# One layer's kernel on one core: shift constants turned on PE, the last table's index made first, half of the h norms turned by DMA, one chain of roots for q, one PSUM ring of four

## The chip, the cores and the metric

The kernel runs on one core of a Trainium2 chip. A core has TensorE (PE, matrix products into PSUM), VectorE (DVE), ScalarE (ACT), GpSimd (POOL) and the queues that issue DMA transfers (SP's above all). Each engine works through its own instructions in order and waits on semaphores for the others. The metric is the device time of one execution in microseconds, smaller is better. Three runs of the kernel before gave 247.6 to 248.36 us, median 248.21 us.

## The reference

There are 2048 positions of 512 values. Stage A is a gated long convolution, stage B a mixer with an MLP. Everything is bf16 with sums in fp32.

```python
def _A_ref(q, k, v, shift_k, ssm_k, ssm_D):        # q comes in layer-normed
    for t in range(4):                              # four taps along the positions
        k_shift += k_pad[:, t:t + S, :] * shift_k[:, 3 - t]
    kv = k_shift * v
    y = irfft(rfft(kv, 2S) * rfft(ssm_k, 2S))[:S]   # a convolution of length 2048 for each channel
    return q * (y + kv * ssm_D)

h = x + _A_ref(_layernorm(x), k, v, ...)            # x is A_q

def _B_ref(x, w1, w2, w3, w4):                      # x is _layernorm(h)
    g = _gelu(_layernorm(x) @ w1)                   # 512 -> 512
    hs = shifted_by(-1, +1, -2, +2)(g quarters) @ w2
    x1 = x + hs
    return x1 + _gelu(_layernorm(x1) @ w3) @ w4     # 512 -> 1792 -> 512
out = h + _B_ref(_layernorm(h), ...)
```

## The kernel before, in words

The convolution is done as a Fourier transform written as matrix products. The channels come in two halves, cc = 0 and 1. The steps, with the names that the profile uses:

- **Front.** k, v and the long kernel (h, `hraw`) are loaded (`load_k`, `load_v`, `load_h`; 512 KB each, four of each) on SP's queue. PE first runs products of zeros (`pz`, `warm_up`) until k is there. `k_transposed` turns k on PE (`pk`) and an evacuation copies it to `kT`. `k_taps` applies the four taps on PE (`psh`) against diagonal matrices `dg`, and DVE multiplies by v on the way out (`kvq`, line 457). `k_rows` moves `kvq` by DMA into rows (`Rk`, line 464). `h_layout` turns the long kernel (`pt`, line 478), evacuated into `s` (`Rh`). `stage_a` is the first transform (`pah` of the kernel, `pak` of kv, line 494), evacuated into `T` (tile `ab`).
- **Tables.** POOL writes index grids (iota), POOL or DVE turn them into phases (`phase`), ACT takes sines. `WA` and `CSG` are small tables; `Wc` is a block-diagonal table, zeroed by 12 POOL memsets (line 385) and filled by 4 DMAs (line 388); `Wf` is the last table, made from an index `uf` (lines 394 to 398), which lies in the memory of `q_sb`, so q is loaded after the sines of `Wf` have read it (`qfree`, line 402; q loads at line 406). `Wf2` is `Wf` with its halves exchanged (`turned`, line 556).
- **Middle.** `stage_c` (`pc`, lines 518 to 520, three matmuls for each of 128 columns) needs all of `T` of its half and `Wc`. Its 32 PSUM tiles are evacuated into `s` (`xt`), DVE multiplies the transforms (`product`, line 641, and the sums at 655 and 657 into `Yr`, `Yi`). Then 16 groups of `pg` (line 721) go back, evacuated into `ab` (`Gs`). An evacuation can run on ACT or DVE (`evac`, lines 172 and 174). In between DVE takes the statistics of q (line 601, 16 instructions) and their inverse roots in two chains of eight columns each (`rsqrt_q`, `newton`).
- **Swap.** When all `Gs` are out, the PSUM pools of the front (rings `psa` and `psb`, two buffers each, taken in turn) close, and `psY` (2 buffers), `psT` (1) and `psW` (3) open. This is `mid`.
- **Tail.** `last_level` (`py`, line 774, eight) is evacuated by ACT, multiplied by the normed q and added to q by DVE (`gate`, lines 783 and 785), then statistics, roots (`rsqrt_h`) and norms (`norm_h`, line 812 on ACT, 815 on DVE) for blocks b = 0 to 3 of four position tiles. `on_pe` turns the normed tiles on PE (`pt2`, line 828, eight transposes for each pair) and an evacuation writes `xT`. Then w1 with GELU (`pw`, lines 840 and 844), w2 (`p2`, line 912), x1, statistics, roots, norms, again turned (`on_pe` for b = 0, `dma_start_transpose` at line 945 on SP's queue for the others), w3 with GELU, and w4 (`p4`, line 979) with the final sum (line 984) and the stores (line 989). Products of zeros (`pv`, `keep`) stand between the `py`.

The order is written out by hand: every step is added to a plan with a number, and `ISSUE` is the list of the numbers in the order in which they are issued, with a letter (A, V, G) where a step may run on more than one engine. Each engine keeps its part of this order. The plan's costs are not used when the kernel is built. Every DMA takes one of eight completion semaphores in turn and waits, at its place in its queue, until the last DMA of the same semaphore has landed.

Of the kernel before, what the change touches and what calls it, by code (L numbers as in the profile page):

```python
# [16 lines left out]
P = 128  # L17
S = 2048
# [5 lines left out]
DC = D // P  # L24
# [18 lines left out]
19 21 2 26 0 1 28 84 23 20 27 85 9 6 3 7 86 11 88 5 29 14 15 24 36 12 8 10 38 83 37 44 39 40 45 41 42 30G 31 17  # L43
22 25 81 87 46 43 32 18 95 34 16 47 92 96A 97V 94A 51 98 93V 89 105 91V 35 100A 54 49 133 99V 13 52 55 50 67 90A
101 33 134 48 63 136 106 102 138 103 104 4 56 64G 53 135V 137A 113 108 114 109 110 107 146 147A 58 116 57 141
156 142V 148 150 151V 157A 152 149A 153A 158 160 139 68G 161A 65 159V 143 261 154 69 112 140A 117 70 155V 115
111 118 166 145 167V 263 59 66 162 125 176 61 163A 62 174 366 177A 178 126 179A 164 172 175V 173V 182 165A 170
168 121 169V 122 183A 260 188 171A 189A 72 60 264 265A 76 75 73 221 220 74 215 218 219 216 214 217 230 231 232
233 80 79 190 228 192 191A 78 271 193A 272A 269 124 270A 186 127 266 184 267A 119 273 128 276 268 77 129 187A
185A 120 234 130 71 278 277A 281 279A 283 235 293 275 180 274 282A 284A 222 229 288 236 290 280 237 285 181A 295  # L50
289A 291A 123 238 287 239 294A 286 302 144 240 292 305 241 296A 210V 312 297 306V 242 262 303A 131 243 225 132
196 197A 202 200 208 201A 198 203A 199V 224 227 194 209A 204 195A 244 307 206 300 205A 207A 301A 223 226 318
308A 299 320 319A 298 313 315 245 304 309 310 321A 330 246 314A 332 311 316A 211A 247 325 327 322 331A 385 333A
317 248 328A 326A 367 324 323 373V 334 344 345A 342 337 343A 339 375V 329 338A 249 354 340A 336 356 351 335 250
349 346 371V 355A 341 374V 357A 352A 399 348 420 361 82 363 347 350A 395 369V 400A 251 396A 397 386 391 398A 358
393 353 360 359 212V 394V 387 392A 417 418V 388A 403 213V 252 404A 376V 405 406A 407 389 390V 409 408A 415 411
401 410A 416V 412A 402V 413 414A 419 446 253 254 440 255 368 256 257 258 259 454 441 370V 372A 379V 447A 377A
378A 448 449 450 452 455A 456 453 457 451 458 460 384A 459 461 499 500A 462 463 424 428 491 464 381A 492A 427
493 465 501 466 494 365 467 380A 438 495 468 496 469 470 502 471 472 503 505 477V 433 506 497 544 504 545A 498
507 508 430 473 383A 581 435 436 536 509 510 511 512 513 514 515 516 517 582A 425 434 537A 538 423 445 589 421  # L60
444 546 522V 439 478A 547 539 548 542 540 550 549 541 431 543 551 481 552 518 476A 475A 482A 362 426 553 554 442
432 382A 474 422 443 479 555 583 437 556 480A 429 489 520A 521A 524 487 485 523A 490 525A 364 519 488 486 557
558 559 770 560 526 527A 561 562 590A 584 483 568V 591 585 587 566V 586 592 588 593 484 595 594 532 596 597 598
599 528 533 600 629 529 530 601 567A 563 531 534 535 602 603 564 571 604 635 630 605 631 606 637 572A 565A 569
607 636 610V 570A 644 642 613V 632 633 634 638 640 639 645 643 641 646 647 648 649 650 651 573 579 574 577 575
652 653 580 611A 614 578 608 576 654 667 668 612A 655 669 615A 616 656V 617A 659V 664 666 657V 618 665 672 624
622 619 676 674 670 625 620 673 671 677 675 658A 662 623 678 679 626 680 621 609 699 681 663A 682 660 628 683
627 684 696 697 685 702 686 687 701 700 703 698 708 706 704 709 707 705 710 661A 781 782 779 773 780 774 688A
791 711 712 713 714 715 792 716 689 690A 717 785 787 731 691 718 719 732 733 771 738 739 786 740 789 741 752
692A 753 788 728 730 693 694A 695 790 772 754 724A 722A 797 798 726A 736 737 775 776 720A 755 729 734 817 818  # L70
756 757 825 826 758 759 827 828 725 829 735 833 830 834 760 742 823 824 723 761 743 777 778 793 794 766V 727 821
822 795 831 796 744 832 815 813 816 745 814 811 746 768V 812 783 784 721 747 819 835 836 820 805 800 853 847 748
859 749 854 848 809 860 810 871 750 851 751 762V 872 764V 852 769 861 804 799 867 763 873 862 868 869 767 874
# [59 lines left out]
def kernel(  # L133
# [23 lines left out]
    psa = front.enter_context(tc.tile_pool(name="psa", bufs=2, space=bass.MemoryType.PSUM))  # L157
    psb = front.enter_context(tc.tile_pool(name="psb", bufs=2, space=bass.MemoryType.PSUM))
    X = {"psa": psa, "psb": psb}
    plan = Plan({"psa": 2, "psb": 2, "psY": 2, "psT": 1, "psW": 3})  # L160
# [63 lines left out]
    def uf(hf):  # L224
        return X["q_sb"][:, 4 * hf:4 * hf + 4, :].rearrange("p a b -> p (a b)").bitcast(I32)
# [3 lines left out]
    ssk_bf = cst.tile([P, DC, 4], BF16)  # L229
# [20 lines left out]
    add({"A": 0.6}, lambda: nc.scalar.dma_start(ssk_bf[:], A_shift_k.rearrange("(c p) j -> p c j", p=P)), w=["sskb"], x=(0.6, 3.4))  # L250
# [5 lines left out]
    dma(0.6, lambda: nc.sync.dma_start(dcol[:], A_ssm_D.rearrange("(c p) -> p c", p=P)), w=["dcol"], x=(0.8, 2.5))  # L256
# [34 lines left out]
    add({"V": 0.5}, small, w=["warm", "mpi", "zero"])  # L291
    add({"V": 0.1}, lambda: V.memset(kT()[:, :, 26:32, 0:2], 0.0), r=("AB",), w=["kz"])
    add({"A": 0.3}, lambda: A.activation(warm[:], warm[:], ACT.Sin), r=["warm"], w=["sin"])
# [8 lines left out]
    def numbers():  # L302
# [10 lines left out]
    add({"V": 1.5}, numbers, r=["pidx"], w=["pf"], lock=True)  # L313
    v(2.2, lambda: V.tensor_tensor(
        out=dg().rearrange("p c j s -> p (c j) s"), in0=ident[:].unsqueeze(1).to_broadcast([P, 4 * DC, P]),
        in1=ssk_bf[:].rearrange("p c j -> p (c j)").unsqueeze(2).to_broadcast([P, 4 * DC, P]), op=MUL),
      ["id", "sskb", "AB"], ["dg"], lock=True)
# [33 lines left out]
    def hold():  # L351
        add({"G": 0.2}, lambda: G.tensor_tensor(out=gt[:], in0=CSG[:, 0:4], in1=dg()[:, 0, 0, 0:4], op=ADD),
            ["dg", "CSG"], ["gate"])
# [8 lines left out]
    sine(0.5, lambda: trc()[:, 1], uw, "uW", ("t", 1), False, ["AB"])  # L362
    add({"V": 0.2}, lambda: V.tensor_scalar(trc()[:, 2], trc()[:, 1], -1.0, None, op0=MUL),
        ["AB", ("t", 1)], [("t", 2)], lock=True)
    cosine(0.5, lambda: trc()[:, 0], uw, "uW", ("t", 0), ["AB"])
    for lo, hi, mult, off, key in ((0, 64, p64, 0.0, "uA"), (64, 81, k2X, 2048.0, "uG"), (81, 96, k2X, 0.0, "uH")):
        v(0.08, lambda lo=lo, hi=hi, mult=mult, off=off: V.tensor_scalar(
            um()[:, lo:hi], um()[:, lo:hi], mult, off, op0=MUL, op1=ADD), ["AB", "pf"], [key], lock=True)
    v(0.1, lambda: V.tensor_scalar(um()[:, 0:96], um()[:, 0:96], ANG - 1, None, op0=OP.bitwise_and),
# [5 lines left out]
    v(0.08, lambda: V.tensor_scalar(mk[:], i4[:], d4X, 1.0 / S, op0=OP.is_equal, op1=MUL), ["pf", "pidx"], ["mk"], lock=True)  # L375
    v(0.2, lambda: V.tensor_tensor(out=CSG[:].rearrange("p (n d) -> p n d", d=4),
# [3 lines left out]


    hold()
    for q in range(4):
        for a in range(3):
            add({"G": 0.95}, lambda q=q, a=a: G.memset(
                X["Wc"][:, q, a].rearrange("p d n k -> p (d n k)").bitcast(U32), 0), ["W", "gate"], [("wz", q, a)])
# [6 lines left out]
    for hf in range(2):  # L393
        iota(1.05, lambda hf=hf: uf(hf), [[1, 16], [32, 64]], 16 * hf, ("uf", hf), ["S1", "gate"])
        phase(0.75, lambda hf=hf: uf(hf), k1F, offF, ("uf", hf), ["S1"],
              after=[("wz", q, j) for q in range(4) for j in range(3)])
        sine(1.15, lambda hf=hf: Wf[:, 0, 16 * hf:16 * hf + 16, :].rearrange("p a b -> p (a b)"),
             lambda hf=hf: uf(hf), ("uf", hf), ("Wf", 0, hf), True, ["S1"])
# [3 lines left out]
    freed("qfree", [("uf", 0), ("uf", 1)])  # L402
    qd = A_q[0].rearrange("(n h t) d -> h n t d", h=2, t=NT)
    for tq in range(4):
        for h in range(2):
            dma(0.43, lambda h=h, tq=tq: nc.sync.dma_start(
                X["q_sb"][h * N1:(h + 1) * N1, 4 * tq:4 * tq + 4, :], qd[h][:, 4 * tq:4 * tq + 4, :]),
                r=["qfree"], w=[("q", h, tq)], x=(1.12, 2.5))

    def warm_up(n, x):  # L410
        key = ("pz", x)

        def pe():
            pz = psum("psb", key)
# [3 lines left out]
        add(mm(n), pe, ["zero"], [key, ("pzd", x)], opens=("psb", key))  # L418

    def k_transposed(qr):  # L420
# [10 lines left out]
        for cc in range(2):  # L431
            add({"A": 1.0, "V": 0.61},
# [593 lines left out]
```

## Time and profile before

| | us |
|---|---|
| median of three runs | 248.21 |
| the profiled execution, its own time | 247.9 |
| its span in the profile | 246.1 |
| PE, DVE, ACT, POOL busy | 229.4, 164.0, 155.5, 18.2 |
| first `pc` matmul | 41.20 |
| first `py` matmul | 95.43 |
| first `pw` matmul after which PE no longer waits | 118.02 |
| last `ob` sum on DVE (start) | 242.58 |

The span is 1.8 us shorter than the profiled execution's own time. A row of the profile gives start, duration, engine, source line, operation, output from input, and in brackets the idle time before it and who ended it. Instructions of ACT and DVE in a row overlap by about a tenth of a microsecond at their ends, so a row of seven that takes 6.61 us is a pitch of 0.94 us.

### The profile page before, as it was taken

The numbers are of one execution on the slowest core, as the hardware profiler recorded it, in microseconds if no ns is written. First come the engines' busy times: TensorE is split into PE (matmuls) and PEld (weight loads), VectorE is DVE, ScalarE is ACT, GpSimd is POOL, SyncE is SP. The second block draws the span as 40 slices with busy tenths as digits, with TensorE's granted clock in tenths as the row PEclk, the third lists the DMA queues.
The fourth block names the chain that finished last, engine by engine and source line by source line (L and its number), as shares of the span: only waits on it lengthen the run. The fifth ranks groups of instructions, "written<-read, shape, count | busy, mean of one in ns | idle before, by whom it ended". The sixth has DMA issues, their size and how long they took to land.

```text
span 246.1 us, 5097 instructions
## 1 busy us (share of the span) xinstructions
PE 229.4 (93%) x2108; PEld 151.0 (61%) x2108; DVE 164.0 (67%) x391; ACT 155.5 (63%) x203; POOL 18.2 (7%) x32
## 2 busy tenths in 40 slices
PE   8899899998798888988999999999999999999994
PEld 8899788997798875565445544444444444444542
DVE  6736878999999999999999999950150033003411
ACT  6704878999999999999956767863026402730000
POOL 4679100000000000000000000000000000000000
PEclk9999899999999999999999999999999999999999
DMA  6996868710000299000000004440120001101103
GB/s 196 376 407 163 239 198 184 166 50 4 0 3 0 65 355 348 8 0 0 3 0 0 4 1 86 85 87 3 27 48 10 3 15 28 43 3 43 32 21 75
DMA packets 18870, 20.77 MB, mean 84 GB/s; under 512 B 8608, under 2 KB 15392, under 8 KB 18848
## 3 DMA queue, kind: packets, MB, share of 16 engines
q1 hardware_dynamic: 18080, 20.32, 28.2%
q8 instruction: 16, 0.26, 0.5%
q10 hardware_dynamic: 768, 0.14, 0.3%
q14 instruction: 6, 0.05, 0.1%
HBM read 13.11 MB, written 2.10 MB: 62 GB/s over the span
## 4 chain that ended last, share of the span: by engine, by line
PE 63%; ACT 19%; DVE 12%; issue 2%; DMA 2%; SPq 0%; ACTq 0%
PE pw L840 23%; PE p L979 20%; ACT s L172 8%; ACT ab L172 5%; PE p L912 5%; PE psh L453 5%; PE pt L478 3%; DVE ab L174 3%; DVE kin L641 2%; PE pz L416 2%; ACT act L172 2%; DVE bst L597 2%; ACT ab L812 2%; DMA q_sb<-in_A_q_dram 2%; ACT act L844 1%
## 5 line engine op out<-in xcount | busy, mean ns | idle before, releaser
L840 PE MATMUL pw<-act,wts 128*128 128x512 bf16 x288 | 64.3, 379 | 1.1 <-ACT act L172 1.1
L844 ACT ACTIVATE ab<-pw 128x512 bf16<-128x512 f32 x56 | 32.8, 596 | 45.3 <-PE pw L840 34.9
L984 DVE TENSOR_TENSOR wts<-p,wts 128x1024 bf16<-128x1024 f32 (+2 forms) x10 | 10.1, 1011 | 62.0 <-PE p L979 62.0
L840 PEld LDWEIGHTS <-wts 128*128 128x128 bf16 x288 | 28.0, 98 | 34.7 <-issue 1.5
L979 PE MATMUL p<-wts,ab 128*128 128x512 bf16 (+1 forms) x238 | 49.2, 366 | 0.0
L979 PEld LDWEIGHTS <-ab 128*128 128x128 bf16 x238 | 23.3, 98 | 25.3
L518 PE MATMUL pc<-ab,Wc 128*128 128x256 bf16 x128 | 31.0, 282 | 2.0 <-ACT s L172 1.6
L172 ACT CAST s<-pc 128x1024 bf16<-128x1024 f32 x31 | 29.3, 1051 | 0.4 <-DVE kin L641 0.3
L520 PE MATMUL pc<-ab,Wc 128*128 128x128 bf16 x128 | 29.0, 227 | 0.0
L519 PE MATMUL pc<-ab,Wc 128*128 128x128 bf16 x128 | 28.0, 219 | 0.0
L519 PEld LDWEIGHTS <-Wc 128*128 128x128 bf16 x128 | 19.3, 151 | 2.0 <-issue 1.8
L518 PEld LDWEIGHTS <-Wc 128*128 128x128 bf16 x128 | 19.3, 151 | 0.5
L641 DVE TENSOR_TENSOR kin<-s 128x2048 bf16<-128x2048 bf16 x16 | 19.2, 1222 | 0.3
L520 PEld LDWEIGHTS <-Wc 128*128 128x128 bf16 x128 | 18.3, 143 | 0.0
L453 PE MATMUL psh<-ab 128*128 128x128 bf16 x256 | 16.4, 226 | 0.0
L172 ACT CAST ab<-pah 128x1024 bf16<-128x1024 f32 x13 | 12.9, 1038 | 4.6 <-PE pah L494 4.6
L453 PEld LDWEIGHTS <-ab 128*128 128x128 bf16 x256 | 15.4, 102 | 0.5 <-issue 0.2
L912 PE MATMUL p<-wts,act 128*128 128x512 bf16 x64 | 15.5, 379 | 0.1
L457 DVE TENSOR_TENSOR kvq<-psh,kin 128x1024 bf16<-128x1024 f32 x8 | 9.7, 1223 | 7.5 <-DMA kin<-in_A_v_dram 4.5
L172 ACT COPY act<-pt 128x1024 bf16<-128x1024 bf16 x10 | 10.1, 1011 | 2.8 <-PE pt L828 2.8
L172 ACT CAST ab<-pak 128x1024 bf16<-128x1024 f32 x11 | 10.7, 1103 | 1.4 <-PE pak L494 1.4
L918 DVE SCALAR_TENSOR_TENSOR s<-ab,rho,p 128x512 bf16<-128x512 bf16 x16 | 11.6, 740 | 0.0
(138 smaller groups left out, 334.7 us busy)
## 6 DMA issues: line engine op xcount, KB each, us to landing
wts<-in_B_w_dram SPq DMA_DIRECT2D x2, 1792.0 KB, 10.9
kin<-in_A_k_dram SPq DMA_DIRECT2D x4, 512.0 KB, 6.0
ab<-in_A_ssm_k_dram SPq DMA_DIRECT2D x4, 512.0 KB, 9.3
kin<-in_A_v_dram SPq DMA_DIRECT2D x4, 512.0 KB, 10.0
kin<-kvq SPq DMA_DIRECT2D x16, 128.0 KB, 3.6
q_sb<-in_A_q_dram SPq DMA_DIRECT2D x8, 256.0 KB, 5.0
out_dram<-wts SPq DMA_DIRECT2D x14, 128.0 KB, 2.3
Wc<-ab SPq DMA_DIRECT2D x4, 384.0 KB, 4.1
```

The lines of the kernel that those rows point to most:

```text
L172: A.copy(o, src)
L453: T_.matmul(pv[:, g, i, :], lhsT=row(g, 4 * qr + i - j), rhs=dg()[:, 2 * g + cc, j, :], start=(j == 0), stop=(j == 3))
L518: T_.matmul(pv[:, kk], lhsT=W[0], rhs=T[:, :, 2 * k1:2 * k1 + 2, :], start=True, stop=False)
L519: T_.matmul(pv[:, kk, :, 0, :], lhsT=W[1], rhs=T[:, :, 2 * k1 + 1, :], start=False, stop=False)
L520: T_.matmul(pv[:, kk, :, 1, :], lhsT=W[2], rhs=T[:, :, 2 * k1, :], start=False, stop=True)
L641: v(1.13, lambda: V.tensor_tensor(out=prs(), in0=xs(0).unsqueeze(1).to_broadcast([P, 2, 2, 512]), in1=xs(1).unsqueeze(2).to_broadcast([P, ...
L840: T_.matmul(ps[:], lhsT=wt(w)[:, k, m * P:(m + 1) * P], rhs=xT()[:, k, 4 * b * P:(4 * b + 4) * P], start=(k == 0), stop=(k == DC - 1))
L844: add({"A": 0.49}, lambda: A.activation(dst(), X[pkey][:], ACT.Gelu_apprx_tanh), r + [pkey, "gelu"], [key])
L912: T_.matmul(ps[:, i, :], lhsT=gT()[:, m, t + i + 2 + off[m], :], rhs=wt("w2")[:, m, :], start=(m == 0), stop=(m == 3))
L918: v(0.66, lambda t=t, i=i, key=key: V.scalar_tensor_tensor(out=qn()[:, t + i, :], in0=hn()[:, t + i, :], scalar=rho[:, t + i:t + i + 1], i ...
L979: T_.matmul(ps[:, i, x0:x1], lhsT=g2(b % 2)[:, m, s0:s0 + P], rhs=wt("w4")[:, m, x0:x1], start=(m == 0), stop=(m == FC - 1))
L984: v(0.58 * (hi - lo) * (x1 - x0) / D, lambda j=j, lo=lo, hi=hi, x0=x0, x1=x1, key=key: V.tensor_tensor(out=obb()[:, j, lo:hi, x0:x1], in0= ...
```

## The change: what it does

1. The tap constants and `ssm_D` are loaded in rows on four partitions (two DMAs on ACT's queue) in place of two loads of single elements (one on ACT's, one on SP's queue). PE turns them with five small matmuls against the identity (`columns`), DVE copies them out, and the diagonals `dg` are made in two halves.
2. The index of the last table, `uf`, now lies in the memory of `Rk` for cc = 1 and is made before the zeros of `Wc`; a small POOL copy (`gt2`) waits for it and the zeros wait for that. q no longer waits for the sines of `Wf`. The first rows of cc = 1 wait for them.
3. For b = 2 and 3 the normed h tiles are turned by eight `dma_start_transpose` on SP's queue, in place of four `on_pe` groups and their evacuations.
4. One chain of inverse roots for all 16 columns of q; and in every chain one instruction less (the shift and the subtraction become one instruction).
5. One PSUM ring of four buffers in place of two rings of two.
6. k is evacuated in one instruction for each of the four groups, in place of two; three of the `pz` groups have four products in place of eight.
7. `ISSUE` is another list: all steps are ordered and given to ACT and DVE anew.

```diff
-    psa = front.enter_context(tc.tile_pool(name="psa", bufs=2, space=bass.MemoryType.PSUM))
-    psb = front.enter_context(tc.tile_pool(name="psb", bufs=2, space=bass.MemoryType.PSUM))
+    psa = front.enter_context(tc.tile_pool(name="psa", bufs=4, space=bass.MemoryType.PSUM))
...
     def uf(hf):
-        return X["q_sb"][:, 4 * hf:4 * hf + 4, :].rearrange("p a b -> p (a b)").bitcast(I32)
+        return X["kin"][:, 20480 + 2048 * hf:22528 + 2048 * hf].bitcast(I32)
...
-    add({"A": 0.6}, lambda: nc.scalar.dma_start(ssk_bf[:], A_shift_k.rearrange("(c p) j -> p c j", p=P)), w=["sskb"], x=(0.6, 3.4))
+    add({"A": 0.42}, lambda: nc.scalar.dma_start(
+        raw()[:, 0:4, :].rearrange("c j p -> c (j p)"), A_shift_k.rearrange("(c p) j -> c (p j)", p=P)), r=["S2"], w=["rawj"], x=(0.15, 2.3))
+    add({"A": 0.42}, lambda: nc.scalar.dma_start(raw()[:, 4, :], A_ssm_D.rearrange("(c p) -> c p", p=P)), r=["S2"], w=["rawD"], x=(0.15, 2.3))
...
-    dma(0.6, lambda: nc.sync.dma_start(dcol[:], A_ssm_D.rearrange("(c p) -> p c", p=P)), w=["dcol"], x=(0.8, 2.5))
...
+    def columns():
+        ps = psum("psa", "pss")
+        for j in range(5):
+            lhsT = raw()[:, 0:4, :].rearrange("c j p -> c (j p)")[:, j:4 * P:4] if j < 4 else raw()[:, 4, :]
+            T_.matmul(ps[:, 4 * j:4 * j + 4], lhsT=lhsT, rhs=ident[0:DC, 0:DC], start=True, stop=True)
...
+    for cc in range(2):
+        def diagonals(cc=cc):
+            V.tensor_tensor(out=dg()[:, cc:DC:2], in0=ident[:].unsqueeze(1).unsqueeze(1).to_broadcast([P, 2, 4, P]),
+                            in1=ssk[:, :, cc:DC:2].rearrange("p j g -> p g j").unsqueeze(3).to_broadcast([P, 2, 4, P]), op=MUL)
...
+    for hf in range(2):
+        iota(1.05, lambda hf=hf: uf(hf), [[1, 16], [32, 64]], 16 * hf, ("uf", hf), ["C", "gate"])
+        phase(0.68, lambda hf=hf: uf(hf), k1F, offF, ("uf", hf), ["C"])
+    gt2 = cst.tile([P, 2], I32)
...
-    freed("qfree", [("uf", 0), ("uf", 1)])
+    freed(("Rfree", 1), [("uf", 0), ("uf", 1)])
+    freed(("Rfree", 0), [])
...
-                r=["qfree"], w=[("q", h, tq)], x=(1.12, 2.5))
+                r=["S1"], w=[("q", h, tq)], x=(2.0, 2.0))
...
-        yield lambda: V.tensor_scalar(r.bitcast(I32), vv.bitcast(I32), 1, None, op0=OP.logical_shift_right)
-        yield lambda: V.tensor_scalar(r.bitcast(I32), r.bitcast(I32), -1, 0x5F1FFFF9, op0=MUL, op1=ADD)
+        yield lambda: V.tensor_scalar(r.bitcast(I32), vv.bitcast(I32), -0.5, 0x5F1FFFF9, op0=MUL, op1=ADD)
...
-    rsqrt_q(0, 8, 0)
-    rsqrt_q(8, 16, 1)
+    rsqrt_q(0, 16, 0)
...
-            for i in (0, 2):
-                on_pe(lambda j, t=4 * b + i: hn()[:, t + j, :], 4 * b + i, [("hn", 4 * b + i), ("hn", 4 * b + i + 1), "HH"])
+            if b < 2:
+                for i in (0, 2):
+                    on_pe(lambda j, t=4 * b + i: hn()[:, t + j, :], 4 * b + i, [("hn", 4 * b + i), ("hn", 4 * b + i + 1), "HH"])
+            else:
+                for t in range(4 * b, 4 * b + 4):
+                    dma(1.2, lambda t=t: nc.sync.dma_start_transpose(xT()[:, :, t * P:(t + 1) * P], hn()[:, t, :]),
+                        r=["C", "HH", ("hn", t)], w=[("xT", t)], x=(1.0, 0.15))
```

In the new order, from the first `pc` to the last `Gs`, ACT has 53 evacuations (28 of `pc`, 6 of `pah`, 7 of `pak`, 12 of `pg`), where before it has 55 (31, 6, 7, 11) and besides a table load and one part of `Wf2`. DVE evacuates all four `pt` (two before), eight of its 16 statistics of q come before its first `pc` evacuation (none before), and it has four evacuations of `pc` (one before). All eight `kvq` come before the first `pc` evacuation (seven before). Loads of q stand between the `kvq` rows and the `Wc` fills on SP's queue.

More of the change, by code (lines that the diff above doesn't have):

```diff
@@ L48 @@
[L48 to L52, printed above, removed]
@@ L611, in rsqrt_q @@
               [lambda: V.scalar_tensor_tensor(out=vv, in0=m0, scalar=-0.5, in1=rr, op0=MUL, op1=MUL)],
[L612 to L615 removed]
+              [("bst", t) for t in range(lo, hi)], [("rq", 0), ("mvq", 0)], False)
+    rsqrt_q(0, 16, 0)
     def Y():
@@ L715 @@
         key = ("pg", i)
-        ring = ("psa", "psb")[i % 2]
+        ring = ("psa", "psa")[i % 2]
         def pe(i=i, key=key, ring=ring):
```

137 lines of the change are left out of this document (71 added, 66 removed), and 7 rows, old and new, of the table ISSUE.

## The prediction

> **What bounds the kernel now.** I read the page first: busy times and the strip of 40 slices.
>
> ```profile
> PE 229.4 (93%) x2108; PEld 151.0 (61%) x2108; DVE 164.0 (67%) x391; ACT 155.5 (63%) x203; POOL 18.2 (7%) x32
> ...
> PE   8899899998798888988999999999999999999994
> ...
> DVE  6736878999999999999999999950150033003411
> ACT  6704878999999999999956767863026402730000
> ```
>
> PE looks like the bound everywhere, but DVE and ACT are full in slices 7 to 20 and PE is not. So I read the busy times by stage (columns: stretch, its length, then PE, PEld, DVE, ACT, POOL, granted clock, DMA).
>
> ```profile
> 50.00:60.00 10.00, 9.40 (x124) 9.12 (x123) 9.85 (x21) 9.99 (x12) 0.00 (x0) 1.00 0.09 28
> 60.00:70.00 10.00, 8.23 (x126) 7.56 (x125) 9.84 (x16) 10.00 (x12) 0.00 (x0) 1.00 0.01 2
> 70.00:80.00 10.00, 9.14 (x116) 9.06 (x115) 9.84 (x18) 9.95 (x11) 0.00 (x0) 1.00 0.00 0
> ...
> 95.40:118.00 22.60, 20.19 (x206) 12.12 (x207) 21.63 (x75) 21.76 (x29) 0.00 (x0) 1.00 0.11 43
> 118.00:153.00 35.00, 34.80 (x195) 16.82 (x195) 33.84 (x133) 25.23 (x39) 0.00 (x0) 1.00 0.08 16
> ```
>
> There are three regimes: up to 41.2 a front of PE, loads and evacuations; from 41.2 to 95.4 ACT and DVE both at 98% or more; from 118 PE without a stop. The timeline of ACT shows the middle:
>
> ```profile
> 60.35 6.61 ACT L172 CAST ab<-pak 128x1024 bf16<-128x1024 f32 x7
> 66.89 5.63 ACT L172 CAST s<-pc 128x1024 bf16<-128x1024 f32 x6
> 72.55 1.06 ACT L562 ACTIVATE kvq<-Wf 64x1024 bf16<-64x1024 bf16 x1
> 73.63 7.46 ACT L172 CAST s<-pc 128x1024 bf16<-128x1024 f32 x8
> 81.42 3.77 ACT L172 CAST s<-pc 128x1024 bf16<-128x1024 f32 x4 [0.32 <-DVE kin L641]
> 85.04 10.23 ACT L172 CAST ab<-pg 128x1024 bf16<-128x1024 f32 x11
> ```
>
> One evacuation follows the other at a pitch of 0.935 us, and 0.26 us after the last the first py starts. The timeline of PE shows where the turned h norms lie in the tail:
>
> ```profile
> 118.02 3.61 PE L840 MATMUL pw<-act,wts 128*128 128x512 bf16 x16 [0.42 <-ACT act L172]
> 121.47 0.61 PE L828 MATMUL pt<-ident,ab 128*128 128x128 bf16 x8
> 121.92 1.89 PE L912 MATMUL p<-wts,act 128*128 128x512 bf16 x8
> ```
>
> A turn moves the next matmul by 0.45 us. The DMA that is to replace it exists already, for x (ns to issue, then us to landing):
>
> ```profile
> L945 SPq DMA_TRANSPOSE act<-act x12: 1190/1217/1302, 146.3 to 163.7; - x12
> ...
> DMA to landing us min/median/max: 2.4/2.5/3.1
> ```
>
> **The change part by part.** The sum is made against the profiled execution: span 246.1, own time 247.9 us, 0.3 below the median of 248.21.
>
> *Shift constants.* Removed: the load of single elements (4.6 us to landing; DVE waits 1.04 us for it at line 314) and dcol's (9.6 us; POOL waits 2.0 us). Added: two loads of rows on ACT's queue, five small matmuls, two DVE copies (0.15 to 0.3 us each). No row load of this size is shown; the nearest are ACT's stores of 32 KB, 2.0 us, and the old load, 4.6 us. I take 2.3, being nearer in kind; they land at about 3.5. The identity no longer waits on POOL behind a phase (0.78 us) and is there at 2.5 in place of 3.5; that phase moves to DVE (0.42). DVE reaches the copies at about 5.0, and the diagonals (2.29 in all) end at 7.6 against 7.92. With the slow load they end at 8.8. The first taps run at 10.6, so both ends cost nothing.
>
> *Fewer zeros.* 20 fewer products of about 0.08 us each: PE is done at 4.5, but k lands at about 5.9 (PE waits 0.4 for it now), so nothing is gained.
>
> *Index first.* POOL makes uf at about 8 to 12.6 and then zeros Wc, 12 times 0.92 us, to 24; before, zeros and index were mixed and ended at 25.6. The fills follow on SP's queue behind eight kvq rows and one load of q, at 27 to 31 (26.0 before), and land 4.1 us later, by 35. The first pc is at 41, a cover of 6 us. The sines of Wf move to about 11 to 14, where ACT now idles 5.72 us; the table load (1.28) also leaves the middle. q no longer waits for the sines, so eight statistics of q move into DVE's idle time before 42.
>
> *The front's end.* SP now sends three h loads ahead of v, not two: 512 KB more at 400 GB/s, +1.3 us; but dcol and the element load (1 us at 200 GB/s in place of 400) are gone. The second v landed at 16.1; bounds 15.5 and 18.7, I take 17.5. From there DVE runs two kvq, two Rh, two kvq at 1.14 each, to 23.5. The ring of four ties PE to that: a tile waits for the one four before. PE then does two pt groups (1.95), six pah (0.45), two psh (1.9) and two pak (0.36), to 33.5, one more psh, to 35.4, and then ACT has six evacuations of 0.935 until T of the first half is whole: 41.5. First pc at 41.6 against 41.2: **+0.4**, bounds -0.9 (v as early as it can be) to +3 (v at its bound, and a half-clock stretch as below).
>
> *The middle.* ACT before: 55 evacuations of 0.935, 1.28 of table load and 1.06 of Wf2, 53.8 us, from 41.3 to 95.17. After: 53, or 49.6 us. DVE before: 53.2 us. After: eight statistics fewer (-4.8), three pc evacuations more (+3.4), no kvq (-1.1), one pg less (-1.1), one half of Wf2 more (+0.4), ten small root instructions fewer at 0.09 (-0.9), three norms of q fewer (-1.0): 48.1. DVE can start on the second pc tile, at 43.9, and end at 92.0. PE needs 44 us in this stretch (pc 128 columns of 0.245, pg 7.4, pah and pak 4.5, zeros 0.9) and is under both. From ACT's 91.1 and DVE's 92.0 I put the first py at 92.3 against 95.43; with the front's +0.4 the middle alone is **-3.5** (bounds -4.2, ACT's count, and 0, stops that eat it all).
>
> *The tail to 118.* Steps are counted from the first py. The first block's roots end at 12.0 before (107.43); after, one chained instruction of 0.2 less and one gate after them instead of before: 11.2. First pw at 17.0 (17.2 before); PE without waits from 22.3 (22.6). The eight q norms on DVE (0.32 each) lie under ACT's last pg evacuations. **-0.3.**
>
> *h norms by DMA.* Four turns leave PE: 4 x 0.45 = **-1.8**; four evacuations leave ACT, where they were hidden. But a turn stood between the last pw of a block and the p2 that needs its GELU. Without it p2 waits: 0.7 in the first block, 0.3 in the second, and 0.4 more around the x turns. And the transposes are in a row on SP's queue, 1.2 us each: block 2's last norm ends on ACT at about 27.35 (behind four GELUs), its DMA lands at 30.1, and PE is ready at 29.9. Block 3's land at 37.0, PE is ready at 37.4. With semaphore delays the waits are about **+1.1**; bounds 0 and +3.4 (landing 3.1 and issue 1.3 in both blocks). The x transposes queue behind these, at 46 or later, no conflict.
>
> *Roots elsewhere* are shorter by 0.2 us in each chain, inside DVE's time: no gain of their own. After this PE does the same matmuls, and the end (last sum, store) is the same.
>
> Sum: +0.4 - 3.5 - 0.3 - 1.8 + 1.1 = **-4.1**: span 242.0, own time 243.8; with the 0.3 to the median, 244.1 us.
>
> **The rivals.**
> - *The front comes late (slower).* DVE has now 28 us of work between 7.6 and the first pc: four pt evacuations, eight kvq, eight statistics. All of it hangs on v, and every microsecond of v moves the first pc by as much. For: loads of v took 9.2 to 11.3 us, v's issues wait on earlier landings, the last v landed at 22. It decides from a first pc at 45.7; with v at 22 for the first kvq pair, as the last v now, it is at 46.1 and with one stretch at half clock 47.8. Time about 249.8. Against: the bytes ahead of the last v are the same.
> - *A stretch at half clock.* The windows of 28 to 32 us show it:
>
> ```profile
> 28.00:30.00 2.00, 2.00 (x31) 1.71 (x30) 1.17 (x3) 1.22 (x2) 0.00 (x0) 0.59 1.08 338
> 30.00:32.00 2.00, 2.00 (x23) 2.00 (x22) 1.04 (x1) 2.00 (x2) 0.00 (x0) 0.56 1.09 348
> ```
>
>   It costs 1.7 us of PE (32 psh took 2.92 in place of 1.96) and followed 0.8 us of idle PE at 24.7 to 27. The new front has such gaps at 17, 22 and after 4.5. One stretch more on the path: 245.8. [...]
> - *The transposes give the tail back.* Landing 3.1, issue 1.3, and block 2's last norm one GELU and one norm later: +2.7 over the forecast, 246.8. For: PE's margin is 0.2 us. Against: 2.5 is the median.
> - *The saved work becomes waiting.* One ring, first in first out: a pc tile that DVE holds behind a product (1.13) stops PE and then ACT. The middle keeps its length: +3.5, 247.6. For: DVE now has four pc tiles. Against: PE has 5 us to spare, and two rings of two also wait on their own older tile.
> - *Better:* v as early as it can be and no waits for the transposes: 241.8.
>
> **How the numbers follow.** Forecast 0.42, late front 0.15, half clock 0.10, transposes 0.15, waiting 0.12, better 0.06. A measurement of this kernel tells 0.3% (0.75 us) from no change. Faster: the forecast, half clock, transposes, better, and a third of waiting: 0.77; same 0.08; slower 0.15. The likeliest time is 244.1, its own range 242.6 to 245.6. The range takes in the transposes and waiting: 241.5 to 248.6.
>
> **What would show it.** First pc at 40 to 44; ACT with hardly an idle gap between the last pak of the first half and the last pg, 49 to 50 us; first py at 91.5 to 93.5; last transposes of each h block landing within 0.5 us of PE's need; six turns at 0.45 on PE, and holes before p2 of 0.3 to 0.7. It is wrong if the first pc is after 45, if ACT in the middle waits for PE by several microseconds, or if w1 of blocks 2 and 3 waits for a DMA by more than a microsecond each.

## The result, and the profile after

The changed kernel is slower: 251.42 us (median of four, 250.82 to 252.16) against 248.29 (247.6 to 248.81) for the kernel before on the same chip, a ratio of 1.0129 with a 95% interval of 1.0085 to 1.0173. The forecast was 244.1. The profiled execution took 251.99 us, its span is 250.2 (before 247.9 and 246.1).

Busy times and strip of the changed kernel, which answer to the first lines shown of before (40 slices of 6.3 us; PEclk is the granted clock in tenths):

```profile
PE 227.5 (91%) x2057; PEld 149.7 (60%) x2069; DVE 164.7 (66%) x372; ACT 147.4 (59%) x194; POOL 17.6 (7%) x31
...
PE   7559999999899966987969999999999999999994
...
DVE  6543896999999999999999989860043034003321
ACT  5470268989999999799955856866006501640000
...
PEclk9967999999999999999999999999999999999999
```

PE and ACT do less than before (227.5 and 147.4 us against 229.4 and 155.5), and still the span is longer. The second to fourth slices show where: PE is half idle in the second and third, and its clock is at 0.6 and 0.7 in the third and fourth. The timeline of PE gives the places:

```profile
10.37 0.22 PE L475 MATMUL psh<-ab 128*128 128x128 bf16 x1
15.40 6.48 PE L475 MATMUL psh<-ab 128*128 128x128 bf16 x63 [4.81 <-ACT ab L170]
...
25.54 3.75 PE L475 MATMUL psh<-ab 128*128 128x128 bf16 x64
...
48.42 0.33 PE L540 MATMUL pc<-ab,Wc 128*128 128x256 bf16 x1
...
99.73 0.62 PE L794 MATMUL py<-ab,Wf 128*64 128x512 bf16 x4 [1.12 <-ACT ab L170]
```

The taps begin, stop after one product for 4.81 us, and then 63 of them take 6.48 us, where 64 took 3.90 before. The three stages, from the first `pc`, the first `py` and the end of the span in the two profiles:

| | before | after | difference |
|---|---|---|---|
| front, to the first `pc` | 41.20 | 48.42 | +7.2 |
| middle, to the first `py` | 54.23 | 51.31 | -2.9 |
| tail, to the end of the span | 150.67 | 150.47 | -0.2 |
| span | 246.1 | 250.2 | +4.1 |

So the gain in the middle came, at -2.9 of the -3.5 forecast, and the front lost more than twice as much. PE waits for an ACT write to `ab`. The instructions that write it are the evacuations of k (ACT and DVE timelines of the changed kernel):

```profile
9.28 0.37 ACT L364 ACTIVATE WA<-ab,mpi 128x64 bf16<-128x64 f32 x1 [3.90 <-DVE ab L172]
...
10.27 1.87 ACT L170 COPY ab<-pk 128x2048 bf16<-128x2048 bf16 x1
13.48 1.87 ACT L170 COPY ab<-pk 128x2048 bf16<-128x2048 bf16 x1 [1.35 <-DVE ab L172]
```

```profile
8.02 1.22 DVE L172 COPY ab<-pk 128x2048 bf16<-128x2048 bf16 x1
12.17 1.23 DVE L172 COPY ab<-pk 128x2048 bf16<-128x2048 bf16 x1 [2.93 <-ACT ab L170]
```

They run strictly by turns, DVE, ACT, DVE, ACT, from 8.02 to 15.35, and a sine of the small table `WA` (line 364), which reads its scratch in the same tile, stands in the same row. In the kernel before, the eight halves ran on both engines side by side (DVE, then ACT):

```profile
8.01 0.69 DVE L174 COPY ab<-pk 128x1024 bf16<-128x1024 bf16 x1
8.99 0.69 DVE L174 COPY ab<-pk 128x1024 bf16<-128x1024 bf16 x1 [0.28 <-ACT ab L172]
10.82 1.29 DVE L174 COPY ab<-pk 128x1024 bf16<-128x1024 bf16 x2 [1.14 <-PE pk L428]
```

```profile
6.96 1.99 ACT L172 COPY ab<-pk 128x1024 bf16<-128x1024 bf16 x2 [0.65 <-PE pk L428]
```

The four groups write different rows, so nothing that is computed asks for such an order. But half 0 of `kT` lies at 0 to 4160 of `ab`, the scratch of the tables at 4160 to 5696, half 1 from 8192 on: an instruction that writes a group's rows in both halves reaches, from its first to its last address, over the scratch and over rows of other groups. That gave theory A: the built program takes the whole reach as written and puts the instructions in a row. The list of semaphore waits in the built program agrees. These are ACT's two merged evacuations in the changed kernel, and the four that stand there when each is split by halves (the writes are the same, only their grouping differs). Merged, the first waits for ACT's own work on the scratch, which waits for DVE's evacuation, and the second waits for DVE's next one; split, only the waits for PE are left:

```
L170 TensorCopy ab<-pk 128x2x8x128 [waits PE_49,Activation_49]
L170 TensorCopy ab<-pk 128x2x8x128 [waits DVE_49,PE_49]

L170 TensorCopy ab<-pk 128x8x128 [waits PE_49]
L170 TensorCopy ab<-pk 128x8x128
L170 TensorCopy ab<-pk 128x8x128 [waits PE_49]
L170 TensorCopy ab<-pk 128x8x128
```

### The profile page after: what moved, and what is told of

Its sections match the earlier page's. It is cut to its first block, busy times and chain, and to the rows that moved or that the text cites. A ratio compares the mean times of both kernels' runs of the same rounds, so it can differ in the third digit from the quotient of the medians.

```text
span 250.2 us, 4998 instructions
## 1 busy us (share of the span) xinstructions
PE 227.5 (91%) x2057; PEld 149.7 (60%) x2069; DVE 164.7 (66%) x372; ACT 147.4 (59%) x194; POOL 17.6 (7%) x31
## 4 chain that ended last, share of the span: by engine, by line
PE 62%; DVE 19%; ACT 13%; DMA 2%; issue 1%; SPq 1%; ACTq 0%
PE pw L860 22%; PE p L1004 19%; PE psh L475 7%; ACT ab L170 5%; PE p L937 4%; DVE kin L661 4%; ACT s L170 3%; PE pt L500 3%; DVE ab L172 3%; DVE bst L618 2%; PE pah L516 2%; PE pc L540 2%; DMA s<-in_A_ssm_D_dram 2%; DVE wts L803 1%; ACT ab L832 1%
## 5 line engine op out<-in xcount | busy, mean ns | idle before, releaser
L864 ACT ACTIVATE ab<-pw 128x512 bf16<-128x512 f32 x56 | 32.8, 596 | 41.9 <-PE pw L860 30.9
L1004 PEld LDWEIGHTS <-ab 128*128 128x128 bf16 x238 | 23.3, 98 | 25.3
L170 ACT CAST s<-pc 128x1024 bf16<-128x1024 f32 x28 | 27.1, 1111 | 1.7 <-PE pc L542 0.9
L475 PE MATMUL psh<-ab 128*128 128x128 bf16 x256 | 18.3, 239 | 4.8 <-ACT ab L170 4.8
L475 PEld LDWEIGHTS <-ab 128*128 128x128 bf16 x256 | 17.1, 108 | 5.3 <-ACT ab L170 5.0
L937 PE MATMUL p<-wts,act 128*128 128x512 bf16 x62 | 14.7, 379 | 0.1
L170 ACT CAST ab<-pak 128x1024 bf16<-128x1024 f32 x14 | 13.3, 1098 | 0.7 <-PE pak L516 0.7
L170 ACT CAST ab<-pg 128x1024 bf16<-128x1024 f32 x12 | 11.3, 1067 | 0.4 <-PE pg L741 0.4
## 6 DMA issues: line engine op xcount, KB each, us to landing
kin<-in_A_v_dram SPq DMA_DIRECT2D x4, 512.0 KB, 10.6
```

Of the source, the lines that this page charges most:

```text
L170: A.copy(o, src)
L475: T_.matmul(pv[:, g, i, :], lhsT=row(g, 4 * qr + i - j), rhs=dg()[:, 2 * g + cc, j, :], start=(j == 0), stop=(j == 3))
L864: add({"A": 0.49}, lambda: A.activation(dst(), X[pkey][:], ACT.Gelu_apprx_tanh), r + [pkey, "gelu"], [key])
L937: T_.matmul(ps[:, i, :], lhsT=gT()[:, m, t + i + 2 + off[m], :], rhs=wt("w2")[:, m, :], start=(m == 0), stop=(m == 3))
L1004: T_.matmul(ps[:, i, x0:x1], lhsT=g2(b % 2)[:, m, s0:s0 + P], rhs=wt("w4")[:, m, x0:x1], start=(m == 0), stop=(m == FC - 1))
```

## The experiments

The rivals were B, the one on record (v and DVE's chain make the front late), C (making the index first makes the `Wc` fills late), and later D, F and G, told below. All ratios are to the kernel before on the same chip.

### k split again in the changed kernel

```diff
-            lambda e: evac(e, kT()[:, :, 8 * qr:8 * qr + 8, 2:KP],
-                           X[key][:].rearrange("p (c y s) -> p c y s", c=2, s=P)),
+            lambda e: [evac(e, kT()[:, cc, 8 * qr:8 * qr + 8, 2:KP],
+                            X[key][:].rearrange("p (c y s) -> p c y s", c=2, s=P)[:, cc]) for cc in range(2)],
```

> The changed kernel with one thing undone: each k evacuation is again two instructions, one per channel half, on the same engine and at the same place. Theory A (the merged instruction spans both halves, so the four k evacuations and the table work whose scratch lies between the halves wait for each other in turn): the four evacuations run on ACT and DVE side by side, PE's stop of 4.8 us before the taps goes, first pc at 41 to 43 instead of 48.4, median 244 to 246.5 us. Theory B (the front is late through v and DVE's chain, the rival on record): first pc stays at 46 or later, 249.5 to 252 us. Theory C (making the index first sends the Wc fills out late, and they are what pc waits for): the taps come early, but the first pc waits for a DMA, at 44 to 47, 247 to 250 us.

Measured: 245.85 us, ratio 0.9927 (0.9895 to 0.9958): with this one edit the changed kernel is faster than before. PE's timeline:

```profile
10.40 3.74 PE L475 MATMUL psh<-ab 128*128 128x128 bf16 x64
...
18.42 3.73 PE L475 MATMUL psh<-ab 128*128 128x128 bf16 x64 [0.56 <-DVE kvq L479]
...
43.89 0.33 PE L540 MATMUL pc<-ab,Wc 128*128 128x256 bf16 x1
```

The stop and the half clock at 15 to 21 are gone (granted clock 1.00 from 8 to 22); the first `pc` comes 4.5 us earlier. That is theory A in time and place, and B's 46 or later did not come. C would have the first `pc` wait for a DMA; PE goes over to it from the product before with no idle time. But 43.89 is over A's 41 to 43 and 2.3 over the forecast's 41.6: something else is left in the front, taken up below.

### The merge alone, in the kernel before

```diff
         for cc in range(2):
-            add({"A": 1.0, "V": 0.61},
-                lambda e, cc=cc: evac(e, kT()[:, cc, 8 * qr:8 * qr + 8, 2:KP], ...[:, cc]),
+            add({"A": 1.87, "V": 1.15},
+                lambda e, cc=cc: evac(e, kT()[:, :, 8 * qr:8 * qr + 8, 2:KP], ...) if cc == 0 else None,
```

> The kernel before with only the merge: one k evacuation instruction over both halves, at the place and on the engine of the first half's; the second half's is empty. Theory A: here too the four wait for each other (1.9 us on ACT, 1.2 on DVE, one after the other), taps and first pc come 3 to 7 us later, 251 to 255 us. Theory B and C: four instructions fewer, first pc within 1 us of 41.2, 247.5 to 249 us.

Measured: 248.65 us, ratio 1.0037 (1.0012 to 1.0061), first `pc` 41.87: a miss by size. The evacuations do run by turns here too (7.31 to 14.4), but it costs 0.7 us. PE and DVE of this kernel show why:

```profile
11.38 2.01 PE L453 MATMUL psh<-ab 128*128 128x128 bf16 x33
14.46 1.91 PE L453 MATMUL psh<-ab 128*128 128x128 bf16 x31 [1.07 <-ACT ab L172]
```

```profile
15.93 2.35 DVE L457 TENSOR_TENSOR kvq<-psh,kin 128x1024 bf16<-128x1024 f32 x2 [3.28 <-DMA kin<-in_A_v_dram]
```

In this order the first tap group is issued ahead of the last two evacuations and runs between them; PE stops for 1.07 us only and keeps its clock (1.00 from 8 to 32); and DVE waits for v until 15.93 whatever the taps do. The merge is harmful where the order and the slack make it so.

### k still merged, the first two tap groups issued ahead of the last evacuation

In `ISSUE`, `103` and `107` (`psh` of groups 0 and 1) go to just before `102A`:

```diff
-... 52V 27 102A 17 103 53 57 68 13 75 107 ...
+... 52V 27 103 107 102A 17 53 57 68 13 75 ...
```

> The changed kernel, k still merged, with the first two tap groups issued ahead of the last k evacuation in the program (PE's own order is the same). If PE's stop comes from reading rows that the last merged evacuation, as its span goes, covers too, the taps start at about 12 in place of 15.4, without the stretch at half clock, and the first pc comes 2 to 4 us earlier, at 44.5 to 46.5: 247.5 to 249.5 us. If only the length of the chain of four evacuations counts: first pc 48 to 48.8, 251 to 252 us.

Measured: 248.65 us, ratio 1.0019 (0.9999 to 1.004), first `pc` 45.25, as expected of the reach and not of the chain's length alone:

```profile
13.24 5.32 PE L474 MATMUL psh<-ab 128*128 128x128 bf16 x63 [2.49 <-DVE ab L171]
```

In the changed kernel the second product needs group 3, which was copied by 12.14, and yet PE went on at 15.40, after group 2. With the taps issued ahead of it PE no longer waits for group 2, but it still waits for group 1, until 13.24 and not the 12 expected. The expectation that the half clock would go too was wrong: it came after 2.49 us of idle time (granted clock 0.50 from 15 to 17).

### k still merged, the scratch of the tables moved away

```diff
-        return X["ab"][:, 4160:5184].bitcast(I32)
+        return X["ab"][:, 16384:17408].bitcast(I32)
...
-        return X["ab"][:, 5184:5696].bitcast(I32)
+        return X["ab"][:, 17408:17920].bitcast(I32)
```

> The changed kernel with k still merged, but the scratch of the tables moved out of the space between the two halves. It parts theory A in two. If the k evacuations hold each other (A1): they still run one after the other, only the waits between sines and evacuations go; first pc 46 to 48, 249.5 to 251.5 us. If the scratch is what ties them (A2): first pc at 41 to 43.5, 244 to 247 us. Theory B: no change, 251 to 252 us.

Measured: 249.93 us, ratio 1.0076 (1.005 to 1.0102), first `pc` 46.40: A1. ACT's evacuations and DVE's second one:

```profile
9.42 1.87 ACT L170 COPY ab<-pk 128x2048 bf16<-128x2048 bf16 x1 [3.88 <-DVE ab L172]
12.63 1.87 ACT L170 COPY ab<-pk 128x2048 bf16<-128x2048 bf16 x1 [1.35 <-DVE ab L172]
```

```profile
11.32 1.23 DVE L172 COPY ab<-pk 128x2048 bf16<-128x2048 bf16 x1 [1.99 <-ACT ab L170]
```

The row begins 0.85 us earlier, since no sine stands in it any more, and the evacuations still wait for each other. Moving the scratch was worth 2.0 us of the first `pc`, the split 4.5. The rest of the 2.0 goes along with a shorter stretch at half clock: the granted clock of 0.72 from 14 to 20 makes 3.4 us of it, where the changed kernel has 6.9.

### k split, and the zeros at kT's edges split too

```diff
-    add({"V": 0.1}, lambda: V.memset(kT()[:, :, 26:32, 0:2], 0.0), r=("AB",), w=["kz"])
+    add({"V": 0.1}, lambda: [V.memset(kT()[:, cc, 26:32, 0:2], 0.0) for cc in range(2)], r=("AB",), w=["kz"])
```

> The changed kernel with the k evacuations split and the zeroing of kT's edges split too (two memsets, one per half). Theory A: the 1.5 us that POOL's table iota waits for DVE goes as well, index and zeros end about 1 us earlier, the time is 0 to 1 us under that of the kernel with only k split: 243.5 to 246. Theory B: 249.5 to 252. Theory C: 1 us earlier fills move the first pc by 1 us against the kernel with only k split.

Measured: 245.89 us, ratio 0.9912 (0.9878 to 0.9946), first `pc` 43.54. Its interval and that of the kernel with only k split overlap, so the timing shows no gain from this edit. It does not test C either: POOL's wait of 1.5 us is gone, but its zeros of `Wc` end at 28.46 against 28.67 and not a microsecond earlier, because POOL waits for a load of h in between, until 21.1 in one and 21.3 in the other.

### k split, v first

SP's loads go from h1, v2, v0, v1, h3, v3 to v0, v1, h1, h3, v3, v2:

```diff
-... 17 ... 13 ... 9 11 ... 18 ... 16 ...
+... 9 ... 11 ... 17 18 ... 16 ... 13 ...
```

> The changed kernel with k split, and SP's loads in the order of before again: v0 and v1 ahead of the last two h, v2 last (in the changed kernel h1, v2, v0, v1, h3, v3). Theory D: what is left of the late front once k is split (first pc 43.9 against a forecast of 41.6) is the wait for v, since DVE waits 3.5 us for the first and 1.8 us for the second pair of v, and PE's ring stands behind it: first pc at 41 to 42.8, median 243.7 to 245.2 us, against 245.85 with k split alone. Rival: PE and the evacuations set the front by then, v only fills a gap: first pc 43.5 to 44.2, 245.4 to 246.3 us.

Measured: 245.15 us, ratio 0.9860 (0.9833 to 0.9887), first `pc` 41.84, first `py` 93.16. Theory D holds. (The profiled execution with k split alone had a stretch at half clock from 25 to 28.5 (granted clock 0.55, 0.50, 0.50 and 0.74 in the four windows from 25 to 29), but that is not what was gained: the kernel with k split and PE's turns, below, has the same front, ran at full clock (mean granted clock 1.00), and its first `pc` is at 43.71.) The `kvq` of DVE with k split alone, and then with v first as well:

```profile
17.14 2.50 DVE L479 TENSOR_TENSOR kvq<-psh,kin 128x1024 bf16<-128x1024 f32 x2 [3.53 <-DMA kin<-in_A_v_dram]
...
23.68 2.36 DVE L479 TENSOR_TENSOR kvq<-psh,kin 128x1024 bf16<-128x1024 f32 x2 [1.78 <-DMA kin<-in_A_v_dram]
```

```profile
14.63 2.50 DVE L478 TENSOR_TENSOR kvq<-psh,kin 128x1024 bf16<-128x1024 f32 x2 [0.82 <-DMA kin<-in_A_v_dram]
21.44 1.23 DVE L478 TENSOR_TENSOR kvq<-psh,kin 128x1024 bf16<-128x1024 f32 x1 [1.00 <-DMA kin<-in_A_v_dram]
```

### v first, k still merged

The same edit of SP's order, and no other, in the changed kernel.

> The changed kernel with only the order of SP's loads put back (v0 and v1 ahead of the last two h, v2 last); k stays merged. Theory D with A: the late taps (15.4 and half clock) stand ahead of v here, so v's order is hidden: first pc 47.5 to 48.6, 250.8 to 252 us, although the same edit was worth 2 us of the first pc once k was split. Rival B (v alone is what makes the changed kernel's front late): first pc at 46 or earlier, 249.5 us or less.

Measured: 250.41 us, ratio 1.0098 (1.007 to 1.0126, the changed kernel 1.0085 to 1.0173), first `pc` 47.93. The same edit that was worth 2.05 us moves the first `pc` by 0.5 here, into the range expected; the time is 0.4 us under its range. DVE's first `kvq`:

```profile
18.97 1.23 DVE L478 TENSOR_TENSOR kvq<-psh,kin 128x1024 bf16<-128x1024 f32 x1 [3.28 <-PE psh L474]
```

It waits for PE, not for v. That refutes B as the cause of the late front in the changed kernel: the two delays lie one behind the other, and the late taps hide the late v.

### The DMA turns, both ways

The changed kernel with k split, and blocks 2 and 3 turned on PE again, as in the kernel before:

```diff
-            if b < 2:
-                for i in (0, 2):
-                    on_pe(...)
-            else:
-                for t in range(4 * b, 4 * b + 4):
-                    dma(1.2, ... nc.sync.dma_start_transpose(xT()[:, :, t * P:(t + 1) * P], hn()[:, t, :]), ...)
+            for i in (0, 2):
+                on_pe(...)
```

> The changed kernel with k split, and the h norms of blocks 2 and 3 turned on PE again, two turns and two evacuations a block, placed between the matmuls as in the kernel before. By the terms on record (turns -1.8, waits +1.1) it loses 0.7 us against the kernel with k split: 246.3 to 247. Rival F (the DMA turns gave back all that they freed, or more): 244.9 to 245.9 us, and PE's tail from the first py on is as long as with the DMA, or shorter.

And the kernel before with the opposite edit, each DMA right behind its norm, the norms of tiles 8 and 14 earlier on ACT:

```diff
-... 568V ... 566V ... 567A ... 571 ... 572A 565A 569 ... 570A ...
+... 568V 572 ... 566V 570 ... 567A 571 565A 569 ...
-... 610V ... 613V ... 611A 614 ... 612A ... 615A 616 ... 617A ...
+... 610V 614 ... 613V 617 ... 611A 615 612A 616 ...
```

> The kernel before with only the DMA turns of blocks 2 and 3, issued right after each norm. By the terms on record 0.7 us less than before: 247.0 to 247.5. Rival F: 247.7 to 249.5, with PE waiting for a DMA before the first matmul of w1 in block 2 or 3 by over 1 us.

Measured: 246.49 us, ratio 0.9937 (0.9913 to 0.9961) with PE's turns, against 0.9927 (0.9895 to 0.9958) with the DMA's. The median lies in the range that the recorded terms gave (246.3 to 247), but the two kernels ran on different chips. By ratio they differ by 0.001, or 0.25 us, and the intervals are too wide to tell 0.7 us from none. The profiles are finer: the tail from the first `py` to the end of the span is 150.16 us with PE's turns and 150.00 with the DMA's, and 150.47 in the changed kernel's own profile. In these executions the DMA turns are thus worth between 0.2 us gained and 0.3 lost, not the 0.7 gained that was forecast. The kernel before with DMA turns: 250.12 us, ratio 1.0101 (1.0064 to 1.0138), slower, and over both ranges expected. Its waits of PE (sum, times, longest):

```profile
PE pw L839 <- DMA act<-ab: 2.4, 1, 2.4
PE p L916 <- ACT act L843: 1.8, 2, 1.1
```

4.2 us of new waits against 1.8 us of turns freed leaves 2.4, and its tail is 152.94, 2.3 longer than before. The `p2` waits are for GELUs; before them on ACT stand the norms that this edit put earlier, so I count them to the order and not to the DMA (argued, not tried). PE's wait of 2.4 us before w1 of block 2 ends with a DMA's landing, as F had it.

In the changed kernel the same place looks so (PE, and below it the eight transposes: ns to issue as min, median, max):

```profile
122.32 3.61 PE L860 MATMUL pw<-act,wts 128*128 128x512 bf16 x16 [0.24 <-ACT act L170]
125.77 3.62 PE L937 MATMUL p<-wts,act 128*128 128x512 bf16 x15
131.38 3.63 PE L860 MATMUL pw<-act,wts 128*128 128x512 bf16 x16 [1.99 <-DMA act<-ab]
134.84 3.83 PE L937 MATMUL p<-wts,act 128*128 128x512 bf16 x16
```

```profile
L892 SPq DMA_TRANSPOSE act<-ab x8: 1189/1216/2332, 123.9 to 134.4; - x8
...
DMA to landing us min/median/max: 2.4/2.5/3.4
```

No holes before `p2`, none in block 3, and 1.99 us in block 2.

### What holds block 2

Two edits on the kernel with k split and v first. First, the norm of tile 10 on DVE behind that of tile 9, in place of ACT behind the GELUs (`549V` then `550V`, and its transpose second in SP's row):

```diff
-... 549V ... 553 ... 552 ... 550A 555 554 ...
+... 549V 550V ... 553 554 ... 552 ... 555 ...
```

> k split, v first, and the norm of row tile 10 on DVE right behind that of tile 9 instead of on ACT behind four GELUs, its transpose issued at once. If PE's wait for block 2 (1.7 us) comes from the last norm's place on ACT, it falls to 0.3 to 0.8 and the time by about 1: ratio to before 0.979 to 0.984, 243 to 244.3 us. Rival G: DVE's chain of roots for block 3 is late by as much, or the four transposes on SP's queue set the landing: PE's wait or a new one stays at 1.3 us or more, ratio 0.985 to 0.989.

Measured: 244.38 us, ratio 0.9873 (0.9829 to 0.9917): nothing gained. The norms are ready at 118.7, and PE still waits until 124.27:

```profile
124.27 3.63 PE L859 MATMUL pw<-act,wts 128*128 128x512 bf16 x16 [1.80 <-DMA act<-ab]
```

```profile
L891 SPq DMA_TRANSPOSE act<-ab x8: 1189/1217/2130, 116.9 to 127.9; - x8
```

The four issues of block 2 start at 116.9, 119.1, 120.5 and 121.8: the first takes 2.13 us, the others follow 1.3 apart, and the last lands 2.4 later, at 124.2. My reason (the last norm's place on ACT) falls; G's second half holds, the row on SP's queue sets the landing. The same kernel with the zeros of `kT`'s edges split:

> The same with the zeroing of kT's edges split into two memsets. Theory A: POOL's iota no longer waits 1.5 us; the index is not on the path to the first pc, so 0 to 0.5 us under the kernel without it, not told apart from none. Rival C: index and fills set the first pc, 1 us or more.

Measured: 245.0 us, ratio 0.9891 (0.9861 to 0.9921), first `pc` 42.58: no gain, as expected of A. That the first `pc` comes 1.1 us later than without the edit (41.50) goes along with the clock: in this execution the mean granted clock was 0.993, which makes 3.4 us at half clock, and 16 `pah` took 0.91 us at 25.21 and again at 28.36; in the other it was 1.00, and they took 0.73 and 0.71.

Second, block 2's turns on PE and only block 3's by DMA, the two turns between the matmuls of w1 and w2 (in `ISSUE` the norm of tile 10 moves ahead of them too):

```diff
-            if b < 2:
+            if b < 3:
                 for i in (0, 2):
                     on_pe(...)
```

> k split, v first, and of the h norms only block 3 turned by DMA; block 2's two turns are on PE again, between the matmuls as in the kernel before. If the four transposes in a row on SP's queue (first issue 2.1 to 2.3 us, the others 1.3 apart, landing 2.4 after the last) are what holds block 2, PE's wait of 1.7 us goes for 2 x 0.45 us of turns: 0.8 us less, 243.2 to 244.4 us, ratio to before 0.980 to 0.985. Rival: block 3's four now hold PE in the same way, over 0.8 us before its first w1: ratio 0.985 to 0.989.

Measured: 244.31 us, ratio 0.9839 (0.981 to 0.9868), as expected. PE:

```profile
119.11 0.61 PE L847 MATMUL pt<-ident,ab 128*128 128x128 bf16 x8
119.56 1.89 PE L936 MATMUL p<-wts,act 128*128 128x512 bf16 x7
121.60 0.61 PE L847 MATMUL pt<-ident,ab 128*128 128x128 bf16 x8 [0.15 <-ACT act L169]
...
123.77 3.62 PE L859 MATMUL pw<-act,wts 128*128 128x512 bf16 x16
127.22 3.83 PE L936 MATMUL p<-wts,act 128*128 128x512 bf16 x15
```

In the tail no wait of PE for a DMA is left, in block 3 neither: its four transposes have a block's worth of matmuls ahead of them. The tail is 149.42 us against 150.24. The timed intervals of the two kernels overlap, so this step rests on the profiles. This kernel is the best of all and beats both; the changed kernel differs from it in three places:

| | first `pc` | first `py` | tail | span | ratio |
|---|---|---|---|---|---|
| before | 41.20 | 95.43 | 150.67 | 246.1 | |
| changed | 48.42 | 99.73 | 150.47 | 250.2 | 1.0129 |
| k split | 43.89 | 95.20 | 150.00 | 245.2 | 0.9927 |
| k split, v first | 41.84 | 93.16 | 150.24 | 243.4 | 0.9860 |
| k split, v first, block 2 on PE | 41.77 | 93.08 | 149.42 | 242.5 | 0.9839 |

## Why the prediction was wrong, by its own steps

- **The step that failed: the front's end, +0.4, which measured +7.2.** It began at the v loads and took the taps at 10.6 for granted. The merged evacuation of k, in the list of changes, has no term in the sum: it was passed over as two instructions made one, on two engines as before. Of the 7.2 us, 4.5 are the merge (48.42 to 43.89), 2.05 the order of the v loads (43.89 to 41.84), and 0.64 the rest, undone in this order; with k still merged the order of v is worth 0.5. With both put back the first `pc` is at 41.84, the forecast 41.6.
- **v.** The first pair of v was sized well (17.5 taken, 17.14 with k split). The second pair was not asked for at all: it made DVE wait 1.78 us more, until 23.68, where the step had the second pair of `kvq` already done at 23.5. Two slips in the step's own sums nearly cancel: six instructions of 1.14 from 17.5 end at 24.3 and not 23.5, and 35.4 and six evacuations of 0.935 make 41.0, as written, and not 41.5. With both put right the first `pc` is at about 41.9 in place of 41.6.
- **The middle, -3.5, measured -2.9.** The mechanism was right (ACT's count of evacuations at their pitch), and so was the place: 51.31 us in the changed kernel, 51.32 with k split and v first. The rest is ACT's small waits: 0.89, 0.42, 0.19, 0.16 and 0.37 in the changed kernel, 2.03 us, where before had 1.02 and 0.32.
- **The tail to PE without a stop, -0.3, measured 0.0** (22.59 us after the first `py` in both kernels); the first `pw` came 17.0 us after it, as forecast.
- **h norms by DMA, -0.7, measured between 0.2 gained and 0.3 lost.** The 1.8 us freed were right. The waits of 1.1 were put together from holes before `p2`, of which none came, and 0.2 in block 2, where 1.99 came (the pieces named, 0.7, 0.3, 0.4 and 0.2, add up to 1.6 and not to 1.1). The mis-sized piece is the row on SP's queue: 1.2 us was taken for each issue, and the first took 2.33, so that the last landed 31.6 us after the first `py` instead of 30.1.
- **Shift constants**: at no cost, as forecast; the diagonals end at 8.11 (7.6 forecast) and the first tap runs at 10.37.
- **Index first**: at no cost, but the cover of 6 us was not there. The zeros ended at 28.25 in place of 24 (the phases stood behind the k evacuations on DVE, and POOL waited for h), and the fills were issued at 34.9 to 37.7 in place of 27 to 31, behind the late `kvq` rows on SP's queue. They took 4.1 to 9.5 us to land, not 4.1; the last can have landed as late as 47.2, a microsecond ahead of the first `pc`. No row shows PE waiting for them. What slowed them was not tried.
- **The rivals.** The late front had the sign and the place and, with one stretch at half clock, even the size: first `pc` 47.8, measured 48.42. Its mechanism was wrong: in the changed kernel v is not waited for. The half clock came, on the path: about 2.7 us of PE's time (63 products in 6.48 us against 64 in 3.74).

The chain of roots for q, the shift constants and the ring of four were not undone one by one.

## What to carry to other kernels

An instruction that is merged to save its fixed cost (here DVE took 1.22 us in place of twice 0.69, ACT 1.87 in place of 1.99) may be ordered by its whole reach, from its first to its last address, as the four evacuations of k were here: before merging, look at what lies between, who writes there, and which reads are issued behind it. A front of several waits in a row shows only the first one; price each edit again after the one ahead of it is mended. And a row of transposes on one queue landed by its first issue and its length (1.85 to 2.33 us for the first, 1.2 to 1.3 for each one behind it, 2.4 from the last issue to landing), so here it paid to turn by DMA where a block of matmuls stands ahead, and on PE where none does.

## What the runs showed of the hardware

The clock of PE fell after idle times of 0.8 to 4.81 us, and after one of 2.32 us it did not. With k split, PE was idle from 22.80 to 24.96 but for three products, and the windows behind it (columns as in the prediction) are at half clock; in the changed kernel, after 4.81 us of idle time, too:

```profile
25.00:26.00 1.00, 1.00 (x19) 1.00 (x20) 1.00 (x2) 0.11 (x1) 1.00 (x3) 0.55 0.03 12
26.00:27.00 1.00, 1.00 (x20) 0.88 (x19) 1.00 (x2) 0.00 (x0) 1.00 (x2) 0.50 0.64 202
...
29.00:30.00 1.00, 1.00 (x20) 0.93 (x20) 1.00 (x2) 0.06 (x1) 0.00 (x0) 1.00 0.77 244
```

```profile
15.40:17.00 1.60, 1.60 (x16) 1.60 (x17) 0.25 (x1) 1.60 (x2) 1.29 (x3) 0.50 1.03 412
```

Idle times of 2.15 us (k split) and 2.49 us (taps issued early) were followed by half clock, and so was the 0.8 us in the kernel before that the prediction showed (0.59 and 0.18, between 25.1 and 26.7). But the idle time alone does not decide. With k split and PE's turns, PE was idle for 2.32 us, the mean granted clock of the execution was 1.00 (0.993 with k split, where one such stretch came), and the 32 `pt` behind the idle time were followed by 16 `pah` in 0.72 us, where with k split they took 1.07:

```profile
25.09 2.10 PE L499 MATMUL pt<-ident,ab 128*64 128x128 bf16 x32 [2.32 <-DVE kvq L478]
27.12 0.72 PE L515 MATMUL pah<-WA,s 64*128 64x128 bf16 x16
```

What else decides is open. Worked out from the clocks of the windows, the half-clock stretch is 3.4 us long in the kernel before, with k split and with the taps issued early, and 6.9 us in the changed kernel, where it begins while PE is still idle (granted clock 0.73 from 14 to 15).

What such a stretch costs depends on the products in it. With k split, 32 transposing products `pt`, nearly all at half clock, took 2.04 us, against 2.00 (changed kernel) and 2.10 (the first row just shown) at full clock; the 63 taps of the changed kernel took 6.48, against 3.74 for 64. So the 1.7 us that the prediction took for a stretch, half of the 3.4 us worked out for the kernel before, is an estimate of the most that it costs.

The first transpose of the h norms on SP's queue took 2.33 us to issue in the changed kernel, 1.85 with k split, 2.04 with v first as well and 2.13 with the norm of tile 10 on DVE besides; the later ones took 1.2 to 1.3. Being first is not enough for it: in the kernel before, where the twelve x transposes are the first on that queue, none took over 1.30. The cause is open.
